# A sixth staging slot from a ring of x, and loads and small steps reordered, in an attention-plus-feed-forward kernel

## The chip, the cores and the metric

The kernel runs on one core of a Trainium2 chip. The metric is the device time of one execution in microseconds (us). Its engines are TensorE (PE, with weight loads shown as PEld), VectorE (DVE), ScalarE (ACT), GpSimd (POOL) and SyncE (SP), which only issues DMAs. Each works through its own instruction list in the order written; semaphores hold an instruction until what it needs is done.

## The reference

Eight batches, eight heads, 576 tokens, head size 64, all inputs float32. Attention without a score matrix gives x, and x goes through a feed-forward layer of 512 to 2048 to 512 with the activation h + sin(alpha h)^2 / alpha:

```
q_s = exp(q - max(q));   q_s /= sum over the 64 features
k_s = exp(k - max(k));   k_s /= sum over the 576 tokens
kv  = k_s^T @ v                      # 64 x 64 for each head
x   = (q_s @ kv), heads side by side # 4608 tokens x 512
h   = x @ w_in;  s = sin(alpha * h)
out = (h + s * s / (alpha + 1e-9)) @ w_out
```

## The kernel before

Each batch's 576 tokens are nine groups of 64 (the index j). The 4608 tokens of x are worked through as nine tiles of 512 tokens (t from 0 to 8). x stays on chip, transposed, in `xT`, which holds all 4608 tokens.

**A batch.** Its q, k and v are loaded in float32 into slots of the pool `stage`, five of them (`load`, `load_batch`). ACT takes exp of q and k (`exp_q`, `exp_k`, `exp_half`, L118). v is cast to bfloat16 into `vb` (`cast_v`, L137). `kv_mm` multiplies k and v on PE, `kv_norm` scales into `kbd` on DVE. `norm_q` sums q's features on DVE (L145, L150) and multiplies by the reciprocal into `qn` on POOL or DVE (L152). `qn` is transposed on PE (batches 0 and 1) or by DMA (`q_transpose_dma`, from batch 2). `attn_chunk` and `attn_out` multiply with `kbd`, and a cast on ACT or DVE puts x into `xT`.

**A tile.** `mm_h` makes one of 16 slices h of 512 tokens from four matmuls (L253); ACT takes the sine (L259); the square is taken by the engine that a letter in a string names (A for ACT, P for POOL, D for DVE); DVE's `combine` (L269) makes g; `mm_o` (L273) multiplies g with `wout`, and `evac_o` copies and stores. Banks of PSUM are handed out by letters too (`BANKS`). At most four s tiles exist at a time, so a sine waits for the combine four slices before it.

The order on every engine is the order in which the code is written (`tc.manual_schedule()`). All plain loads and stores are issued by SP, weights by POOL, which casts them on the way. A DMA issue on SP waits for the data that it needs and for an earlier DMA, eight issues before it.

**What is special at the start.** Tile 0 is batch 0's first eight groups and tile 1 is batch 1's. While tile 0's output is being multiplied (`o_quad`, four quarters of 16 matmuls, with `take(os, n)` issuing n of them), the code interleaves the attention of batch 1: exp of its two q halves, transposes after 46 output matmuls, `kv_mm` of both halves, `x_half`. The last quarter of `wout` is loaded in two pieces, slices 12 to 13 and 14 to 15; the latter is first needed by the 57th output matmul. The ninth groups of batches 0 and 1 are loaded alone into `q8` and normalized by `norm_q8`; in `o_stream(1)`, the output of tile 1, they are transposed and multiplied (L518 to L527) and become the first 128 tokens of tile 2. The rest of tile 2 is batch 2. Batch 3's v is loaded after batch 2's q transposes and cast by DVE ahead of tile 2's slices.

A dummy copy gates a DMA: a DVE or POOL copy that touches the target makes the load, which follows it on SP, wait; on POOL, a one-element copy `held` from a staged tile makes the weight loads behind it wait until that tile has landed.

Of the kernel before, what the change touches and what calls it, by code (L numbers as in the profile page):

```python
# [23 lines left out]
def kernel(  # L24
# [20 lines left out]
    J = 9  # L45
# [3 lines left out]
    nT = NT // MF  # L49
    BPT = MF // P  # L50
    NB = B * J

    ctx.enter_context(tc.manual_schedule())
    singles = ctx.enter_context(tc.tile_pool(name="singles", bufs=1))
    stage = ctx.enter_context(tc.tile_pool(name="stage", bufs=5))
    att1 = ctx.enter_context(tc.tile_pool(name="att1", bufs=1))
    att2 = ctx.enter_context(tc.tile_pool(name="att2", bufs=2))
    small = ctx.enter_context(tc.tile_pool(name="small", bufs=2))
# [5 lines left out]

    ident = singles.tile([128, 128], F32, name="ident")
    identb = singles.tile([128, 128], BF16, name="identb")
    xT = singles.tile([128, 4, NT], BF16, name="xT")
    q8 = singles.tile([128, 4, 2, D], F32, name="q8")
    win = singles.tile([128, 4, d_ff], BF16, name="win")
    wout = singles.tile([128, nN, dm], BF16, name="wout")  # L70
# [6 lines left out]
    def src_view(t, b):  # L77
        return t[b].rearrange("(i e) (p j) d -> (e p) i (j d)", e=2, j=J)
# [21 lines left out]
    def load_batch(b):  # L100
        load("q", q, b)
        load("k", k, b)
        load("v", v, b)
# [6 lines left out]
    def load_wout(n0, n1):  # L110
        nc.gpsimd.dma_start(out=wout[:, n0:n1, :], in_=wout_v[:, n0:n1, :])
# [27 lines left out]
    def norm_q(b, engs, j1=J):  # L139

        qe = A["qe", b][:, 0:j1].rearrange("p j (ii x d) -> p ii j x d", ii=2, x=2)
        A["qn", b] = qn = att1.tile([128, 2, J, 2 * D], BF16, name="qn")
        qs = small.tile([128, J, 4], F32, name="qs")
        if len(engs) == 1:
            nc.vector.tensor_reduce(qs, A["qe", b].rearrange("p j (i d) -> p j i d", i=4), axis=AXL.X, op=ALU.add)  # L145
            nc.vector.reciprocal(qs, qs)  # L146
        for ii in range(2):
            part = qs[:, 0:j1, 2 * ii:2 * ii + 2]
            if len(engs) == 2:
                nc.vector.tensor_reduce(part, qe[:, ii], axis=AXL.X, op=ALU.add)  # L150
                nc.vector.reciprocal(part, part)
            engs[ii % len(engs)].tensor_tensor(qn[:, ii, 0:j1].rearrange("p j (x d) -> p j x d", x=2), qe[:, ii],  # L152
                                               part.unsqueeze(3).to_broadcast([128, j1, 2, D]), op=ALU.mult)
# [62 lines left out]
    def attn_out(b, ii, half, pool, eng):  # L216
        qT, kt = A["qT", b], kbd[b % 2]
        j0, j1 = XO[half]
        n = (j1 - j0) * P
        xp = pool.tile([128, 2, 512], F32, name="xp", tag="a")  # L220
        for e in range(2):
            nc.tensor.matmul(xp[:, e, 0:n], kt[:, e, ii], qT[:, ii, j0:j1, e * 64:(e + 1) * 64],  # L222
                             start=True, stop=True)
        c0 = (J * b + j0) * P
        eng(xT[:, 2 * ii:2 * ii + 2, c0:c0 + n], xp[:, :, 0:n])  # L225

    def attn_chunk(b, c, j0, j1, xp):
# [18 lines left out]
    def mm_h(t, ni, k0=0, k1=4):  # L246

        if ni == 0 and k0 == 0:
            G[t] = gpool.tile([128, nN, MF], BF16, name="g")
        hp = HP[t, ni] if k0 else bank(BANKS.get(t, 4 * "aabb")[ni])  # L250
        HP[t, ni] = hp
        for ki in range(k0, k1):
            nc.tensor.matmul(hp, win[:, ki, ni * 128:(ni + 1) * 128],  # L253
                             xT[:, ki, t * MF:(t + 1) * MF], start=(ki == 0), stop=(ki == 3))
        return hp

    def sine(t, ni, hp, sq):
# [69 lines left out]
        vv = vb[0].rearrange("p j (i c) -> p i j c", i=4)  # L327
        eng(vv[:, 2 * ii:2 * ii + 2, j0:j1, 0:D], staged["v", 0][:, ii::2, j0:j1])

    GP_CP(singles.tile([128, 1], F32, name="held"), staged["k", 0][:, 0, 0, 0:1])  # L330
    load0(GP, "v", v, 1, 0, 5)
    load0(GP, "v", v, 1, 5, 9)
    for c0, c1 in ((0, 256), (256, 512), (512, 768), (768, 1024), (1024, 1536), (1536, 2048)):
# [42 lines left out]
    for c in range(2, 4):  # L376
        xp = bank("l")
        attn_chunk(0, c, 0, 8, xp)
        DVE_CP(xT[:, c, 0:MF], xp)
    for ki in range(2):  # L380
        for ni in range(2, 4):
            mm_h(0, ni, ki, ki + 1)
    for ni in range(4):
        mm_h(0, ni, 2, 3)

    def h_slot(t, ni, sq, lag):
        hp = mm_h(t, ni, 3 if t == 0 and ni < 4 else 2 if t == 1 and ni < 1 else 0)
        lag.append((t, ni, hp, sine(t, ni, hp, sq)))

    def flush(lag, keep):  # L390
        while len(lag) > keep:
            combine(*lag.pop(0))
# [17 lines left out]


    lag = []
    SQ = "PAPDPAPAPPDPAPAP"
    with ES:
        def load_q1():
            staged["q", 1] = st = stage.tile([128, 4, J, D], F32, name="st_q", tag="st")
            for ii in range(2):
                DVE_CP(st[:, ii, 0, 0:1], zero)
            for ii in range(2):
                nc.sync.dma_start(out=st[:, ii::2, 0:8].rearrange("p i j d -> p i (j d)"),  # L420
                                  in_=src_view(q, 1)[:, ii::2, 0:8 * D])

        def load_kv1():
            for n in "kv":
                staged[n, 1] = stage.tile([128, 4, J, D], F32, name=f"st_{n}", tag="st")
            DVE_CP(staged["k", 1][:, 0, 0, 0:1], zero)
            for ii in range(2):
                for n, t in (("k", k), ("v", v)):
                    nc.sync.dma_start(out=staged[n, 1][:, ii::2].rearrange("p i j d -> p i (j d)"),
                                      in_=src_view(t, 1)[:, ii::2])  # L430

        late = {6: load_q1, 8: lambda: load_wout(8, 12), 10: lambda: load_wout(12, 14), 13: load_kv1}
        for ni in range(nN):
            h_slot(0, ni, "DPPAPPAPPPAPPAPP"[ni], lag)
            flush(lag, 1)
            if ni in late:
                late[ni]()
        flush(lag, 0)

        accs = [bank(kind) for kind in "bbll"]  # L440
        os = o_quad(0, accs, [DVE_CP, ACT_CP, DVE_CP, DVE_CP])
        take(os, 46)
        for ii in range(2):
            exp_half("q", 1, ii, 8)
        norm_q(1, [GP, V], 8)
        load_wout(14, 16)
        for b in range(2):
            nc.sync.dma_start(out=q8[:, :, b], in_=src_view(q, b)[:, :, 8 * D:J * D])
        load_batch(2)

        def cast_v1(ii, eng):
            vv = vb[1].rearrange("p j (i c) -> p i j c", i=4)
            eng(vv[:, 2 * ii:2 * ii + 2, :, 0:D], staged["v", 1][:, ii::2])

        exp_half("k", 1, 0)
        cast_v1(0, ACT_CP)
        exp_half("k", 1, 1)
        q_tile(1)
        for ii in range(2):
            tp = ps_h[0].tile([128, 8, 128], BF16, name="tp", tag="a")  # L460
            q_transpose_ii(1, ii, 0, 8, tp)
            DVE_CP(A["qT", 1][:, ii, 0:8], tp)
        take(os, 4)

        def x_half(ii):
            xp = [bank("a") for _ in range(2)]
            for e in range(2):
                attn_chunk(1, 2 * ii + e, 0, 8, xp[e])
            for e in range(2):
                (ACT_CP, DVE_CP)[e](xT[:, 2 * ii + e, MF:2 * MF], xp[e])  # L470

        kv_mm(1, 0, ps_k, split=True)
        kv_norm(1, 0, 1)
        cast_v1(1, DVE_CP)
        take(os, 4)
        x_half(0)
        exp_to(A["qe", 1][:, J - 2:J], q8)
        take(os, 2)
        kv_mm(1, 1, ps_k, split=True)
        kv_norm(1, 1, 2)  # L480
        take(os, 4)
        x_half(1)
        nc.scalar.activation(zero, zero, AX.Sin)
        take(os)
        for ki in range(2):
            mm_h(1, 0, ki, ki + 1)
        norm_q8()
        load("q", q, 3)
        load("k", k, 3)

        for ni in range(nN):
            h_slot(1, ni, SQ[ni], lag)
            flush(lag, 1)
        cast_v(2, [GP_CP, GP_CP])
        flush(lag, 0)

# [14 lines left out]
    exp_q(2)  # L511
    exp_k(2)
    os = o_stream(1)
    take(os, 10)
    tp = ps_a.tile([128, 2, 2, 128], BF16, name="tp", tag="a")
    for b in range(2):
        for ii in range(2):
            nc.tensor.transpose(tp[:, ii, b], A["qe", 1][:, J - 2 + b, ii * 128:(ii + 1) * 128], identb)  # L518
    DVE_CP(A["qT", 1][:, :, J - 2:J], tp)
    take(os, 7)  # L520
    xp = ps_a.tile([128, 4, 2, P], F32, name="xp", tag="a")
    for c in range(4):
        ii, e = divmod(c, 2)
        for b in range(2):
            nc.tensor.matmul(xp[:, c, b], kbd[b][:, e, ii], A["qT", 1][:, ii, J - 2 + b, e * 64:(e + 1) * 64],
                             start=True, stop=True)
    DVE_CP(xT[:, :, 16 * P:18 * P], xp.rearrange("p c b n -> p c (b n)"))  # L527
    norm_q(2, [GP, V])
    exp_q(3)
    exp_k(3)  # L530
    q_transpose_dma(2, halves=True)
    load("v", v, 3)
    nc.scalar.activation(zero, zero, AX.Sin)
    take(os, 15)
    kv_mm(2, 0, ps_a)
# [14 lines left out]
    DVE_CP(xT[:, :, c0 + 6 * P:c0 + 9 * P].rearrange("p (h c) n -> p h c n", h=2),  # L550
           xp.rearrange("p h (c n) -> p h c n", c=2))
    take(os)
    cast_v(3, [DVE_CP, DVE_CP])
    q_transpose_dma(3)
    load_batch(4)

# [78 lines left out]
```

## Time and profile before

| what | value |
|---|---|
| median of 3 runs | 284.83 us (284.79 to 285.01) |
| the profiled execution | 285.96 us |
| its span, first to last instruction | 284.2 us |
| busy PE, DVE, ACT, POOL | 271.7, 193.0, 225.1, 82.3 us |
| granted PE clock | 1.00 throughout |
| HBM read, written | 36.71 MB, 9.44 MB |

The span is 1.76 us shorter than the profiled execution's own time, and that execution was 1.13 us above the median. In the profile's rows, "out<-in" are the program's tile names, "xN" counts the instructions, and a bracket at the end gives the idle time of the engine just before a row and what ended it. A matmul's shown end is modelled, and neighbouring matmuls overlap. SPq and POOL rows of DMA_DIRECT2D are issues, not transfers.

### The profile page before, as it was taken

How to read it: one execution, taken by the hardware profiler on the slowest of the kernel's cores; microseconds unless marked ns; L12 is line 12 of the kernel's file. 1: busy time of each engine (PE TensorE's matmuls, PEld its weight loads, DVE VectorE, ACT ScalarE, POOL GpSimd, SP SyncE). 2: the span in 40 equal slices, each digit the busy share in tenths (PEclk: the TensorE clock that was granted, in tenths of full speed). 3: DMA queues.
4: the chain of work that ended last, by engine and by line, in shares of the span. 5: the costliest groups of instructions: out<-in, count | busy, mean ns of one | idle time of the engine just before them, and what ended most of it. 6: DMA issues, size and time to landing. Idle time of an engine off the chain costs nothing.

```text
span 284.2 us, 4841 instructions
## 1 busy us (share of the span) xinstructions
PE 271.7 (96%) x1857; PEld 128.0 (45%) x1857; DVE 193.0 (68%) x287; ACT 225.1 (79%) x319; POOL 82.3 (29%) x78
## 2 busy tenths in 40 slices
PE   2899898999999999999999999999999999999995
PEld 1444354445444444444444444444444444444443
DVE  3957868989999768756785677667774555555412
ACT  4978847999479999899989998999877777777500
POOL 2979620674386650025002500341000000000000
PEclk9999999999999999999999999999999999999999
DMA  7999999951999119911991099118011111111143
GB/s 253 302 194 235 295 354 406 307 229 41 242 259 397 47 36 311 348 38 26 278 386 35 9 251 408 36 37 153 9 37 37 37 39 37 37 37 40 43 106 74
DMA packets 39127, 45.80 MB, mean 161 GB/s; under 512 B 17072, under 2 KB 22464, under 8 KB 39104
## 3 DMA queue, kind: packets, MB, share of 16 engines
q1 hardware_dynamic: 33360, 40.57, 45.9%
q0 software_dynamic: 5552, 4.79, 10.2%
q8 instruction: 14, 0.23, 0.3%
q10 hardware_dynamic: 192, 0.14, 0.2%
q14 instruction: 9, 0.07, 0.1%
HBM read 36.71 MB, written 9.44 MB: 162 GB/s over the span
## 4 chain that ended last, share of the span: by engine, by line
PE 71%; DMA 8%; ACT 7%; DVE 7%; issue 3%; POOL 3%; SPq 0%; POOLq 0%; ACTq 0%
PE hp L253 32%; PE op L273 32%; ACT s L259 4%; DMA wout<-in_moe_w_out_dram 3%; DVE g L269 2%; DMA st_v<-in_v_dram 2%; DMA win<-in_moe_w_in_dram 2%; DMA st_k<-in_k_dram 2%; PE xp L222 1%; DVE qs L150 1%; PE op L605 1%; PE lp L253 1%; POOL s L263 1%; DVE vb L137 1%; PE kvp L173 1%
## 5 line engine op out<-in xcount | busy, mean ns | idle before, releaser
L269 DVE SCALAR_TENSOR_TENSOR g<-s,inva_sb,hp 128x512 bf16<-128x512 f32 x128 | 94.3, 745 | 57.3 <-ACT s L261 53.1
L253 PE MATMUL hp<-xT,win 128*128 128x512 bf16 x512 | 128.3, 379 | 0.8 <-DMA win<-in_moe_w_in_dram 0.7
L273 PE MATMUL op<-wout,g 128*128 128x512 bf16 x496 | 124.4, 379 | 0.0
L259 ACT ACTIVATE s<-hp,alpha_sb 128x512 f32<-128x512 f32 x128 | 86.4, 683 | 24.0 <-PE hp L253 22.4
L253 PEld LDWEIGHTS <-win 128*128 128x128 bf16 x576 | 56.1, 98 | 68.3 <-issue 1.3
L273 PEld LDWEIGHTS <-g 128*128 128x128 bf16 x560 | 54.1, 98 | 62.7 <-issue 2.3
L261 ACT ACTIVATE s<-s 128x512 f32<-128x512 f32 x111 | 69.9, 630 | 3.5
L263 POOL TENSOR_TENSOR s<-s 128x512 f32<-128x512 f32 x30 | 32.4, 1095 | 22.3 <-ACT s L259 22.0
L152 POOL TENSOR_TENSOR qn<-qe,qs 128x1152 bf16<-128x1152 bf16 (+1 forms) x12 | 25.1, 2112 | 38.3 <-DVE qs L146 30.2
L285 DVE COPY o<-op 128x512 f32<-128x512 f32 (+2 forms) x33 | 22.1, 669 | 9.7 <-PE op L273 7.4
L137 POOL CAST vb<-st_v 128x1152 bf16<-128x1152 f32 x10 | 11.3, 1164 | 44.3 <-DMA st_v<-in_v_dram 44.3
L118 ACT ACTIVATE ke<-st_k 128x1152 bf16<-128x1152 f32 x16 | 17.9, 1151 | 3.8 <-DMA st_k<-in_k_dram 3.8
L118 ACT ACTIVATE qe<-st_q 128x1152 bf16<-128x1152 f32 (+1 forms) x16 | 17.5, 1129 | 2.5 <-DMA st_q<-in_q_dram 2.3
L145 DVE TENSOR_REDUCE qs<-qe 128x36 f32<-128x2304 bf16 x5 | 12.8, 2554 | 7.9 <-ACT qe L118 7.9
L225 DVE CAST xT<-xp 128x512 bf16<-128x512 f32 (+1 forms) x18 | 13.5, 750 | 0.0
L118 ACT ACT_TABLE_LOAD x7 | 9.0, 1283 | 1.3 <-PEq L619 1.2
L273 PE MATMUL lp<-wout,g 128*128 128x512 bf16 x32 | 8.9, 379 | 0.9 <-DVE g L269 0.9
L273 PE MATMUL hp<-wout,g 128*128 128x512 bf16 x32 | 8.9, 379 | 0.7 <-DMA wout<-in_moe_w_out_dram 0.7
L150 DVE TENSOR_REDUCE qs<-qe 128x16 f32<-128x1024 bf16 (+1 forms) x6 | 7.5, 1244 | 1.8 <-ACT qe L118 1.6
L222 PE MATMUL xp<-qT,kbd 128*128 128x256 bf16 (+1 forms) x40 | 8.2, 286 | 0.5 <-DVE xT L225 0.5
L173 PEld LDWEIGHTS <-ke 64*64 64x64 bf16 x576 | 5.8, 106 | 4.6 <-issue 1.6
L186 DVE TENSOR_TENSOR kbd<-kvp,kvr 64x256 bf16<-64x256 f32 (+1 forms) x20 | 7.4, 369 | 0.5
(83 smaller groups left out, 138.1 us busy)
## 6 DMA issues: line engine op xcount, KB each, us to landing
out_dram<-o SPq DMA_DIRECT2D x70, 128.0 KB, 2.4
st_q<-in_q_dram SPq DMA_DIRECT2D x6, 1152.0 KB, 6.4
st_k<-in_k_dram SPq DMA_DIRECT2D x6, 1152.0 KB, 9.0
st_v<-in_v_dram SPq DMA_DIRECT2D x6, 1152.0 KB, 11.3
st_k<-in_k_dram SPq DMA_DIRECT2D x4, 576.0 KB, 6.4
st_q<-in_q_dram SPq DMA_DIRECT2D x4, 512.0 KB, 6.0
st_v<-in_v_dram SPq DMA_DIRECT2D x3, 576.0 KB, 7.0
wout<-in_moe_w_out_dram POOLq DMA_DIRECT2D x3, 512.0 KB, 10.3
```

Source lines behind the costliest of these rows:

```text
L118: nc.scalar.activation(dst[:, :, ii * 128:(ii + 1) * 128].rearrange("p j (x d) -> p x j d", x=2), src[:, ii::2], AX.Exp)
L137: engs[ii](vv[:, 2 * ii:2 * ii + 2, :, 0:D], staged["v", b][:, ii::2])
L145: nc.vector.tensor_reduce(qs, A["qe", b].rearrange("p j (i d) -> p j i d", i=4), axis=AXL.X, op=ALU.add)
L152: engs[ii % len(engs)].tensor_tensor(qn[:, ii, 0:j1].rearrange("p j (x d) -> p j x d", x=2), qe[:, ii], part.unsqueeze(3).to_broadcast([12 ...
L225: eng(xT[:, 2 * ii:2 * ii + 2, c0:c0 + n], xp[:, :, 0:n])
L253: nc.tensor.matmul(hp, win[:, ki, ni * 128:(ni + 1) * 128], xT[:, ki, t * MF:(t + 1) * MF], start=(ki == 0), stop=(ki == 3))
L259: nc.scalar.activation(s, hp, AX.Sin, scale=alpha_sb[:, ni:ni + 1])
L261: nc.scalar.activation(s, s, AX.Square)
L263: nc.gpsimd.tensor_tensor(s, s, s, op=ALU.mult)
L269: nc.vector.scalar_tensor_tensor(G[t][:, ni], in0=s, scalar=inva_sb[:, ni:ni + 1], in1=hp, op0=ALU.mult, op1=ALU.add)
L273: nc.tensor.matmul(acc, G[t][:, ni, j * 128:(j + 1) * 128], wout[:, ni, :], start=(ni == 0), stop=(ni == nN - 1))
L285: eng(o[:, cols], acc)
```

## The change

- `xT` holds 2560 tokens, five tiles, and is written and read at the column modulo 2560. `stage` gets a sixth slot.
- Batch 3's v is loaded behind its k, ahead of tile 1's slices, and cast by POOL between its products for batches 2 and 3; before, DVE cast it ahead of tile 2.
- Batch 1: q's second half is issued after tile 0's slice 13, with k and v behind it (before, both halves after slice 6). k is no longer gated, since its slot is fresh. The last wout piece waits on POOL until the first half of k has landed.
- `q8` and batch 2's loads are issued after batch 1's q transposes, `q8` behind two DVE copies that touch it; exp of `q8` is moved behind the second `kv_norm`.
- The ninth groups' transposes, products and copies move from tile 1's output into tile 1's slices 11 and 14 (`late_q8`).
- Tile 0: ACT casts the fourth chunk of x, DVE the third; the third-quarter matmuls of slices 0 to 3 are issued with the fourth quarter instead of ahead of it. The squares of slices 9 and 15 go from POOL to ACT and DVE; in tile 1 that of slice 3 from DVE to POOL.

No matmul, activation or transfer is added or left out; four one-element gating copies became six.

```diff
+    NX = 5 * MF
-    stage = ctx.enter_context(tc.tile_pool(name="stage", bufs=5))
+    stage = ctx.enter_context(tc.tile_pool(name="stage", bufs=6))
-    xT = singles.tile([128, 4, NT], BF16, name="xT")
+    xT = singles.tile([128, 4, NX], BF16, name="xT")
...
-        c0 = (J * b + j0) * P
+        c0 = (J * b + j0) * P % NX
...
-                             xT[:, ki, t * MF:(t + 1) * MF], start=(ki == 0), stop=(ki == 3))
+                             xT[:, ki, t * MF % NX:t * MF % NX + MF], start=(ki == 0), stop=(ki == 3))
...
-        DVE_CP(xT[:, c, 0:MF], xp)
+        (DVE_CP, ACT_CP)[c - 2](xT[:, c, 0:MF], xp)
...
-    for ni in range(4):
-        mm_h(0, ni, 2, 3)
...
-        hp = mm_h(t, ni, 3 if t == 0 and ni < 4 else 2 if t == 1 and ni < 1 else 0)
+        hp = mm_h(t, ni, 2 if ni < (4, 1, 0)[min(t, 2)] else 0)
...
-    SQ = "PAPDPAPAPPDPAPAP"
+    SQ = "PAPPPAPAPPDPAPAP"
...
-        def load_q1():
-            staged["q", 1] = st = stage.tile([128, 4, J, D], F32, name="st_q", tag="st")
-            for ii in range(2):
-                DVE_CP(st[:, ii, 0, 0:1], zero)
-            for ii in range(2):
-                nc.sync.dma_start(out=st[:, ii::2, 0:8].rearrange("p i j d -> p i (j d)"),
-                                  in_=src_view(q, 1)[:, ii::2, 0:8 * D])
+        def load_q1(ii):
+            if ii == 0:
+                staged["q", 1] = stage.tile([128, 4, J, D], F32, name="st_q", tag="st")
+            st = staged["q", 1]
+            DVE_CP(st[:, ii, 0, 0:1], zero)
+            nc.sync.dma_start(out=st[:, ii::2, 0:8].rearrange("p i j d -> p i (j d)"),
+                              in_=src_view(q, 1)[:, ii::2, 0:8 * D])
...
-            DVE_CP(staged["k", 1][:, 0, 0, 0:1], zero)
...
-        late = {6: load_q1, 8: lambda: load_wout(8, 12), 10: lambda: load_wout(12, 14), 13: load_kv1}
+        late = {6: lambda: load_q1(0), 8: lambda: load_wout(8, 12), 10: lambda: load_wout(12, 14), 13: lambda: (load_q1(1), load_kv1())}
...
-            h_slot(0, ni, "DPPAPPAPPPAPPAPP"[ni], lag)
+            h_slot(0, ni, "DPPAPPAPPAAPPAPD"[ni], lag)
...
+        GP_CP(held, staged["k", 1][:, 0, 0, 0:1])
         load_wout(14, 16)
-        for b in range(2):
-            nc.sync.dma_start(out=q8[:, :, b], in_=src_view(q, b)[:, :, 8 * D:J * D])
-        load_batch(2)
...
             DVE_CP(A["qT", 1][:, ii, 0:8], tp)
+        for b in range(2):
+            DVE_CP(q8[:, 0, b, 0:1], zero)
+        for b in range(2):
+            nc.sync.dma_start(out=q8[:, :, b], in_=src_view(q, b)[:, :, 8 * D:J * D])
+        load_batch(2)
...
-        exp_to(A["qe", 1][:, J - 2:J], q8)
         take(os, 2)
         kv_mm(1, 1, ps_k, split=True)
         kv_norm(1, 1, 2)
+        exp_to(A["qe", 1][:, J - 2:J], q8)
...
         load("k", k, 3)
+        load("v", v, 3)
+
+        def late_q8(ni):
+            if ni == 11:
+                tp = ps_k.tile([128, 2, 2, 128], BF16, name="tp", tag="a")
+                for b in range(2):
+                    for ii in range(2):
+                        nc.tensor.transpose(tp[:, ii, b], A["qe", 1][:, J - 2 + b, ii * 128:(ii + 1) * 128], identb)
+                DVE_CP(A["qT", 1][:, :, J - 2:J], tp)
+            elif ni == 14:
+                xp = ps_k.tile([128, 4, 2, P], F32, name="xp", tag="a")
+                for c in range(4):
+                    ii, e = divmod(c, 2)
+                    for b in range(2):
+                        nc.tensor.matmul(xp[:, c, b], kbd[b][:, e, ii],
+                                         A["qT", 1][:, ii, J - 2 + b, e * 64:(e + 1) * 64], start=True, stop=True)
+                DVE_CP(xT[:, :, 16 * P:18 * P], xp.rearrange("p c b n -> p c (b n)"))
 
         for ni in range(nN):
             h_slot(1, ni, SQ[ni], lag)
             flush(lag, 1)
+            late_q8(ni)
...
-    take(os, 10)
-    tp = ps_a.tile([128, 2, 2, 128], BF16, name="tp", tag="a")
...
+    take(os, 17)
     norm_q(2, [GP, V])
     exp_q(3)
     exp_k(3)
+    cast_v(3, [GP_CP, GP_CP])
     q_transpose_dma(2, halves=True)
-    load("v", v, 3)
...
-    cast_v(3, [DVE_CP, DVE_CP])
     q_transpose_dma(3)
```

More of the change, by code (lines that the diff above doesn't have):

```diff
@@ L328, in cast_v0 @@
         eng(vv[:, 2 * ii:2 * ii + 2, j0:j1, 0:D], staged["v", 0][:, ii::2, j0:j1])
-    GP_CP(singles.tile([128, 1], F32, name="held"), staged["k", 0][:, 0, 0, 0:1])
+    held = singles.tile([128, 1], F32, name="held")
+    GP_CP(held, staged["k", 0][:, 0, 0, 0:1])
     load0(GP, "v", v, 1, 0, 5)
@@ L513 @@
     os = o_stream(1)
-    take(os, 10)
-    tp = ps_a.tile([128, 2, 2, 128], BF16, name="tp", tag="a")
[L516 to L527, printed above, removed]
+    take(os, 17)
     norm_q(2, [GP, V])
```

## Prediction

> **What bounds the kernel now.** I read the page first, then the stretch table, TensorE's waits, the timeline around each wait, and issue-to-landing times in the tile views.
>
> ```profile
> span 284.2 us, 4841 instructions
> PE 271.7 (96%) x1857; PEld 128.0 (45%) x1857; DVE 193.0 (68%) x287; ACT 225.1 (79%) x319; POOL 82.3 (29%) x78
> DMA  7999999951999119911991099118011111111143
> ```
>
> PE is the bound, and the DMA engines are full for the first fifth of the span. No matmul is removed, so only PE's gaps can pay.
>
> ```profile
> 28.00:31.00 3.00, 2.15 (x10) 0.87 (x9) 2.39 (x6) 2.65 (x5) 2.87 (x4) 1.00 1.12 323
> 31.00:46.00 15.00, 14.24 (x145) 6.99 (x145) 11.61 (x20) 8.30 (x10) 3.96 (x4) 1.00 1.11 344
> 46.00:61.00 15.00, 15.00 (x71) 6.81 (x70) 14.16 (x21) 14.23 (x24) 8.58 (x8) 1.00 0.97 355
> 105.00:134.00 29.00, 29.00 (x208) 13.74 (x206) 20.48 (x29) 27.18 (x40) 6.54 (x5) 1.00 0.56 180
> ```
>
> Columns: window and its length, busy PE, PEld, DVE, ACT, POOL, granted clock, DMA share, GB/s. From 105 us on PE has no gap and the clock is full, so the ring's later tiles can only lose. The gaps:
>
> ```profile
> 31.03 1.89 PE L273 MATMUL lp<-wout,g 128*128 128x512 bf16 x8 [0.88 <-DVE g L269]
> 44.66 1.02 PE L273 MATMUL hp<-wout,g 128*128 128x512 bf16 x4 [0.73 <-DMA wout<-in_moe_w_out_dram]
> 89.09 0.43 PE L222 MATMUL xp<-qT,kbd 128*128 128x320 bf16 x2 [0.49 <-DVE xT L225]
> 103.56 1.02 PE L253 MATMUL hp<-xT,win 128*128 128x512 bf16 x4 [0.17 <-DVE g L269]
> ...
> 28.15 4.20 POOL L263 TENSOR_TENSOR s<-s 128x512 f32<-128x512 f32 x4
> 28.30 0.69 ACT L259 ACTIVATE s<-lp,alpha_sb 128x512 f32<-128x512 f32 x1 [1.06 <-DVE g L269]
> ...
> 23.95 0.88 SPq L420 DMA_DIRECT2D st_q<-in_q_dram  x2
> 36.74 0.76 POOL L111 DMA_DIRECT2D wout<-in_moe_w_out_dram  x1
> 78.96 3.05 DVE L137 CAST vb<-st_v 128x1152 bf16<-128x1152 f32 x2 [0.41 <-DMA st_v<-in_v_dram]
> ```
>
> Four matmuls of 512 columns take 0.86 on the chain, 0.216 each, while one alone lasts 0.379 (group mean); a gap therefore costs its idle plus 0.16: 1.04, 0.89, 0.65 and 0.33. A fifth, about 0.30, is before the second chunk of batch 2's x at 74.20. That is 3.2 us in all, the most the change can bring.
>
> **The start of tile 0, 1.04.** The two x casts of chunks 2 and 3 ran one after the other on DVE (15.07, 1.29); now ACT takes the second, and the four third-quarter matmuls no longer run ahead of the first finished h. That h ends 3 x 0.216 = 0.65 earlier and ACT's first sine moves from 17.30 to 16.65, if the cast is done by 16.24 (ACT free at 15.45, cast 0.60). POOL loses squares 9 and 15 (1.04 each): its two wout issues (0.81 and 0.76) follow square 8 at 25.0 and end at 26.6. ACT is 0.65 earlier but has square 9 (0.63), so sine 11 still ends at 26.5; squares 11 and 12 run from 26.6 to 28.7, where before square 12 ended at 28.15 + 2 x 1.04 = 30.2. DVE's 0.75 combine then frees the l bank at 29.5. PE has 8 matmuls ahead of it from 28.26, until 29.99. The gap goes: -1.04. DVE pays 0.69 for square 15 at 30.4, hidden, since PE needs that result at 40.
>
> **q1's second half.** It moves from an issue at 24.36 to behind combine 12, about 29.7, past the two wout issues on POOL and directly ahead of k1 and v1 on SP. Before, the halves landed 6.5 and 8.9 us after issue, k1's first half 6.1 after 31.07, at 37.1. The engines move some 410 KB/us and were full, so the same bytes stand ahead of k1: k1 lands again near 37.1, and q1's half 1.4 us (576 KB) before it, 35.7, if in order of issue; if it shares with the cast-loads it takes twice its 1.28 us from 31.7, 34.3 (31.7 is 2 after the issue; a quiet transfer lands after 2.4). I take 35.0, since both ends are equally near. From there: exp 1.08, sum 1.20, reciprocal 0.25, product 1.23 (that at 7.11, alone on the port), handovers 0.25: 39.0. PE would reach those transposes at 28.26 + 46 x 0.216 + 0.45 for the first eight = 38.65: +0.35. Behind the wait on PE stand all of output quads and kv matmuls; SP has k1 and v1 behind the gate.
>
> The Trainium skill, "DMA: Bandwidth & Descriptors", section "Queues, rings and completion order", says each engine round-robins between queues per packet; alone that would give 34.3 and no stall, -0.35 on my sum. The trace is mixed: the earlier half needed 6.5 us with cast loads beside it.
>
> **wout's last quarter, 0.89.** POOL's new held copy (0.19) waits for k1's first half, 37.1, and then issues it: 37.3 against 36.74; behind it is only tile 1's first square, at 49. Before, it landed 7.9 us later with q8 and batch 2 queued beside it; now these are issued after the transposes of q1, by about 40.5, so it shares with v1's tail alone. Without them I allow 5 to 6 us (the quiet alpha load took 2.4, k1 6.1): 42.3 to 43.3, needed near 43.1 (43.77 before, less 0.7). Gap gone: -0.89; the late end would cost 0.2, and I charge 0.1.
>
> **q8 later.** Its gate stands behind the two qT copies on DVE (0.65 each), 40.3; SP issues at 40.5 and 41.0, with the batch 2 loads and tile 0's outputs behind. It took 10.2 before in the full queue; quiet transfers 2.4. I take 44.0 (3 after its issue, nearest the quiet row, since v1 is almost in). Then ACT: exp 0.72, o copy 0.59, xT cast 0.59, with handover 46.0. From those transposes (39.68) to tile 1's first matmul on that cast (47.24) PE took 7.56, 6.67 without the wout gap, so it wants the cast at 39.0 + 6.67 = 45.7: +0.3, or 0 to 1.3 from landings of 43.7 to 45. Exp of q8 itself is only moved. Sum up to tile 1: -1.04 +0.35 -0.89 +0.1 +0.3 = -1.2, bounds -1.9 to +2.0 (the last in the rivals).
>
> **The ninth groups in tile 1.** Four transposes and eight 64-column matmuls are moved, not added (0.39 and 0.40 busy, some 0.5 of PE). The matmuls at slot 14 need DVE's copy (0.42) queued behind combine 10, which ended at 59.85: ready at 60.3, PE there at about 60.0. That is +0.3, bounds 0 to 0.5. DVE also has the 0.68 xT copy, less 0.69 for square 3 (now POOL's, 1.04, in its 0.8 idle gaps). The last g is ready near 64.4, needed at 64.7: no charge, but without that cover 0.3.
>
> **v of batch 3.** Its load goes from 72.66, on SP behind the q transposes, to behind k3 near 54.5. Batch 2's loads end some 2 us later than before, so q3, k3 and v3 land near 61, 64 and 67; exp of q3 and k3 begin at 67.52 and 69.63, so nothing is late unless the delay passes 5 us. The casts leave DVE (3.05) for POOL (2 x 1.16) between qn of batches 2 and 3: POOL idles 6.0 there, cover enough. DVE's queue at 79 to 89 is shorter by 3.05, so the xT copy that ended the gap at 89.09 comes on time: -0.65. ACT lost 1.32 waiting on g at 82.76; it can run ahead, but ACT is 11.82 of 12 busy at 93 to 105, so of the 0.33 I count 0.2. The chain to the 74.20 gap loses its 0.68 xT copy: -0.2 of 0.30.
>
> One row speaks against POOL's casts: DVE's casts took 1.54 and 1.60 beside POOL, 0.77 alone at 42.45, and the q product 1.97 beside POOL's. The Trainium skill, "SBUF — State Buffer", section "SBUF: two separate sides", calls the pair's shared port an exclusive lock; by it both casts ahead of batch 2's product would cost 2.3 on the transposes. The cast at 78.96 ended at 80.50, 0.62 after POOL's running product (79.88) and ahead of POOL's next squares, so DVE was served first: I add 0 and keep 2.3 as the far bound (285.2).
>
> **Ring and slots.** A write into xT follows the last read of those columns by over four tiles; the sixth slot removes waits. Both 0; if that wait bit, PE from 105 on would show gaps.
>
> **Sum.** -1.2 +0.3 -0.65 -0.2 -0.2 = -1.95, say -1.9. The profiled execution took 285.96 (span 284.2 and 1.76 around it), 1.13 above the median; it would become 284.06, and the median 284.83 becomes 282.9.
>
> **Rivals.** (a) All five gaps go and nothing comes back: -3.2, 281.6. For it: PE's order is otherwise unchanged; against: three new waits with margins under 0.5. (b) The early gains are given back: q1's half lands at 36.6 or q8 at 45.2, leaving +0.3 -0.65 -0.2 -0.2 = -0.75: 284.1. For it: full DMA until 61. (c) Slower: q1's half keeps its old 8.9 from an issue at 29.7 and lands at 38.6. The transposes come at 42.6 and tile 1's cast matmul at 42.6 + 6.67 = 49.3, 2.0 late; less 0.75 later: +1.3, 286.1. It decides from a landing of 37.3 on (37.9 for 0.2%). Against: k1, issued after it, landed at 37.1 with the same bytes ahead. (d) The early v load collides with outputs and frees nothing: -1.2+0.3, 283.9, inside (b).
>
> **Chances.** Forecast 0.52, (a) 0.13, (b) with (d) 0.20, (c) 0.15. A measurement of this kernel tells about 0.2% (0.57 us) from no change. Of (b) a quarter, and of (c) a fifth, fall within it: faster 0.80, same 0.08, slower 0.12. The range 281.6 to 285.0 leaves out (c) and little else.
>
> **What would show it.** Right: no gap at the first lp output matmul nor at the last wout quarter; DVE without vb casts near 79; no xp gap at 89. Wrong: PE waiting over 1 us at the q1 transposes for DVE, ACT waiting on q8 past 45.2, or gaps beyond 105.

## The result, and the profile after

The changed kernel took 284.57 us (median of 14 runs, 284.03 to 284.95) against 285.49 for the kernel before, run beside it (14 runs, 284.79 to 286.86). The ratio is 0.9953, with a 95% interval of 0.9938 to 0.9968: 1.34 us less at the 284.83 of the first table, so 283.5 where 282.9 was forecast, inside the range. The ratio is not the quotient of the two medians: these lie 0.92 apart, which would make it 283.9. In a later set of runs (E13) the ratio was 0.9966 (0.9948 to 0.9984). Executions that were disturbed are left out of all ratios; the profile of one experiment fell into such an execution, so a second run of that kernel is shown for it.

The page and the stretch table of the changed kernel, the rows that answer to those shown of before:

```profile
span 282.8 us, 4815 instructions
PE 270.2 (96%) x1828; PEld 128.3 (45%) x1857; DVE 188.2 (67%) x285; ACT 226.0 (80%) x321; POOL 83.9 (30%) x80
DMA  7999999996589029811991099018011111111143
...
28.00:31.00 3.00, 3.00 (x15) 1.37 (x14) 2.75 (x7) 2.97 (x5) 1.35 (x2) 1.00 1.21 230
31.00:46.00 15.00, 13.98 (x142) 6.70 (x144) 10.74 (x22) 7.45 (x11) 2.86 (x3) 1.00 0.98 301
105.00:134.00 29.00, 28.74 (x185) 13.57 (x174) 20.54 (x30) 27.18 (x40) 6.48 (x4) 1.00 0.57 181
```

DVE is 4.8 us less busy: 3.05 of it are the two v casts that went to POOL, and most of the rest are the x cast that went to ACT (0.69) and a product for `q8` that took 0.69 instead of 1.52. The stretch from 28 to 31 has lost its gap. From 31 to 46 PE is busy for less, 13.98 where it had been 14.24. That alone shows no new wait, for this profile lacks 29 matmul records (1828 for 1857 weight loads), which lowers PE's busy time a little everywhere, from 105 us on too. PE's busy time can therefore not be compared with before; starts of named matmuls can. The timeline's rows at the old gaps and at the new waits:

```profile
29.73 1.89 PE L274 MATMUL lp<-wout,g 128*128 128x512 bf16 x8
43.48 1.04 PE L274 MATMUL hp<-wout,g 128*128 128x512 bf16 x4
87.59 0.43 PE L223 MATMUL xp<-qT,kbd 128*128 128x320 bf16 x2
102.18 1.02 PE L254 MATMUL hp<-xT,win 128*128 128x512 bf16 x4 [0.24 <-DVE g L270]
...
35.38 1.06 ACT L119 ACTIVATE qe<-st_q 128x1024 bf16<-128x1024 f32 x1 [3.86 <-DMA st_q<-in_q_dram]
38.01 1.22 DVE L153 TENSOR_TENSOR qn<-qe,qs 128x1024 bf16<-128x1024 bf16 x1
39.29 0.62 PE L203 MATMUL tp<-identb,qn 128*128 128x128 bf16 x8 [0.75 <-DVE qn L153]
44.20 0.72 ACT L119 ACTIVATE qe<-q 128x256 bf16<-128x256 f32 x2 [1.08 <-DMA q<-in_q_dram]
59.29 0.39 PE L506 MATMUL xp<-qT,kbd 128*128 128x64 bf16 x8 [0.18 <-DVE qT L500]
...
67.83 1.97 DVE L153 TENSOR_TENSOR qn<-qe,qs 128x1152 bf16<-128x1152 bf16 x1
68.53 3.39 POOL L138 CAST vb<-st_v 128x1152 bf16<-128x1152 f32 x2
```

The first three rows have lost the bracket that they had before; the fourth has kept its own. The second group is the chain of q1's second half: ACT waits for its landing, DVE's product ends at 39.23, and PE, which waited 0.75, starts the transposes at 39.29. Two waits are new: this one and the 0.18 at the ninth groups' products.

Counted by stage, from the first output matmul (28.26 before, 28.00 after, and 28.34 in a second profile of the changed kernel, so the start differs between executions) to the last matmul of the kernel:

| from, to | before | after | difference | forecast |
|---|---|---|---|---|
| first output matmul to second `kv_mm` of batch 1 | 15.18 | 15.07 | -0.11 | -1.04 +0.35 |
| to `kv_mm(2)` | 24.64 | 24.31 | -0.33 | -0.89 +0.1 +0.3 +0.3 |
| to `kv_mm(3)` | 14.20 | 13.92 | -0.28 | -0.2 |
| to `kv_mm(4)` | 23.75 | 23.34 | -0.41 | -0.65 -0.2 |
| to the last matmul | 174.37 | 174.38 | 0 | 0 |
| all | 252.14 | 251.02 | -1.12 | -1.93 |

A second profile of the changed kernel gave 251.06. This span of PE's work, "first output to last matmul", is used below for every run, since it leaves out the start. It is not free of it, though: where the output begins late, as in E2b below, the loads behind it have had more time.

### The profile page after: what moved, and what is told of

Same layout as the page of the kernel before. It is cut to its first block, busy times and chain, and to the rows that moved or that the text cites. A ratio compares the mean times of both kernels' runs of the same rounds, so it can differ in the third digit from the quotient of the medians.

```text
span 282.8 us, 4815 instructions
## 1 busy us (share of the span) xinstructions
PE 270.2 (96%) x1828; PEld 128.3 (45%) x1857; DVE 188.2 (67%) x285; ACT 226.0 (80%) x321; POOL 83.9 (30%) x80
## 3 DMA queue, kind: packets, MB, share of 16 engines
q0 software_dynamic: 5552, 4.79, 10.2%
## 4 chain that ended last, share of the span: by engine, by line
PE 79%; ACT 6%; DMA 5%; DVE 3%; POOL 2%; issue 2%; SPq 0%; ACTq 0%; POOLq 0%
PE op L274 37%; PE hp L254 34%; ACT s L260 3%; POOL s L264 2%; DMA st_v<-in_v_dram 2%; DMA st_q<-in_q_dram 2%; DVE g L270 2%; PE xp L223 2%; PE kvp L174 2%; PE op L611 1%; PE op L254 1%; DMA q<-in_q_dram 1%; ACT vb L329 1%; ACT qe L119 1%; SPq L299 0%
## 5 line engine op out<-in xcount | busy, mean ns | idle before, releaser
L274 PE MATMUL op<-wout,g 128*128 128x512 bf16 x478 | 121.6, 379 | 1.4 <-issue 0.6
L264 POOL TENSOR_TENSOR s<-s 128x512 f32<-128x512 f32 x29 | 30.6, 1067 | 20.2 <-ACT s L260 20.0
L138 POOL CAST vb<-st_v 128x1152 bf16<-128x1152 f32 x12 | 14.7, 1258 | 44.5 <-DMA st_v<-in_v_dram 44.5
```

The costliest lines, as they stand in the source:

```text
L138: engs[ii](vv[:, 2 * ii:2 * ii + 2, :, 0:D], staged["v", b][:, ii::2])
L264: nc.gpsimd.tensor_tensor(s, s, s, op=ALU.mult)
L274: nc.tensor.matmul(acc, G[t][:, ni, j * 128:(j + 1) * 128], wout[:, ni, :], start=(ni == 0), stop=(ni == nN - 1))
```

## The experiments

The theory: the gains are PE's removed gaps, and what is missing of the forecast is the new wait on q1's half and the kept gap at 102. The rivals: the loads' order gains nothing by itself and only the sixth slot pays; or the other way round. E1 to E4 ran on one chip, E5, E6, E9 and E10 on a second, E2b, E12, E13 and E14 on a third, each with the kernel before beside it. The changed kernel itself ran only for the result and as E13, so E3 to E10 are compared with it by the ratio and by PE's work in one profile each.

**E1: before, with the edits to tile 0 alone**

```diff
-        DVE_CP(xT[:, c, 0:MF], xp)
+        (DVE_CP, ACT_CP)[c - 2](xT[:, c, 0:MF], xp)
-    for ni in range(4):
-        mm_h(0, ni, 2, 3)
-        hp = mm_h(t, ni, 3 if t == 0 and ni < 4 else 2 if t == 1 and ni < 1 else 0)
+        hp = mm_h(t, ni, 2 if ni < (4, 1, 0)[min(t, 2)] else 0)
-            h_slot(0, ni, "DPPAPPAPPPAPPAPP"[ni], lag)
+            h_slot(0, ni, "DPPAPPAPPAAPPAPD"[ni], lag)
```

> The kernel before with the tile 0 edits alone: the fourth x chunk cast by ACT, the third-quarter matmuls issued with the fourth, squares of slices 9 and 15 off POOL. Gap accounting: the 1.04 us gap at the first lp output matmul goes, but the last wout piece still lands near 44 to 44.6, so PE waits there that much longer (idle 1.1 to 1.8 us instead of 0.73) and the time falls by 0 to 0.6 us (284.2 to 284.8 by the first median). Rival, each gap counts by itself: 1.04 us less, 283.8. Rival, only the early v load pays: the same gap returns at once in the next output quarter and the time does not move.

Measured: 285.51 against 285.46, ratio 0.9995 (0.998 to 1.0009); 251.99 from first output to last matmul. The gap at 31 was gone, and this took its place:

```profile
42.88 0.76 DVE L451 CAST vb<-st_v 128x1152 bf16<-128x1152 f32 x1 [1.62 <-DMA st_v<-in_v_dram]
43.79 0.48 PE L173 MATMUL kvp<-vb,ke 64*64 64x65 bf16 x36 [1.43 <-DVE vb L451]
```

The second half of batch 1's v landed at 42.86, and PE, 1 us earlier than before, waited 1.43 for it. Tile 0's edits alone show no gain: the loads are next. I had expected wout to be the late one; it was v.

**E2: before, with the ring, the sixth slot and batch 3's v early on POOL**

```diff
-    stage = ctx.enter_context(tc.tile_pool(name="stage", bufs=5))
+    stage = ctx.enter_context(tc.tile_pool(name="stage", bufs=6))
...
+        load("v", v, 3)
...
+    cast_v(3, [GP_CP, GP_CP])
-    load("v", v, 3)
-    cast_v(3, [DVE_CP, DVE_CP])
```

> The kernel before with the ring, the sixth slot, batch 3's v loaded behind its k and cast by POOL alone. Gap accounting: the gaps at 31.0 and 44.7 stay, the gap at 89.1 shrinks from 0.65 to about 0.15, the 74.2 gap (0.30) stays because the ninth groups' xT copy is still ahead of the q sums on DVE: -0.5 us, bounds -0.3 to -0.9. Rival, the early v load is what pays: the whole -1.4 us of the change is seen here. Rival, the ring costs: new waits on PE from 105 us on, time the same or up.

Measured: 284.75 against 285.46, ratio 0.9978 (0.9961 to 0.9995). For its profile the kernel ran once more (E2b), without repeats:

> The same kernel as in the second experiment, for its profile. Gap accounting: gaps at 31.0 (about 1.0 us) and at the last wout piece (about 0.9) as before, the one at 89 down to about 0.15, the one at 103 unchanged (0.3 to 0.4). Rival, the whole gain of the change: the early gaps are smaller too.

It took 285.85 in that one execution (span 284.1). The gap at 89 was gone: from `kv_mm(3)` to `kv_mm(4)` PE took 23.33, as in the changed kernel (23.34). The gap at 102 stayed, at 0.40. Its start differed:

```profile
22.54 1.67 PE L254 MATMUL hp<-xT,win 128*128 128x512 bf16 x7 [1.04 <-DMA win<-in_moe_w_in_dram]
44.50 0.48 PE L174 MATMUL kvp<-vb,ke 64*64 64x65 bf16 x36 [0.85 <-DVE vb L454]
```

PE waited 1.04 for w_in in tile 0, its first output matmul came at 29.44, and the gap at 31 did not arise at all; yet v's last half landed at 43.56, 1.9 later than in the profile of before (41.65), and cost 0.85. So the slot with the early v is worth some 0.2% by itself (0.63 us), and the start differs by more than that from one execution to the next (28.26 and 29.44).

This limits what can be said of the rivals. PE's work in E2b was 250.83, less than the changed kernel's 251.02, though its order at the start is that of before. The first two stages of the table together took 39.82 before, 39.38 and 39.44 in two profiles of the changed kernel, and 39.03 in E2b. E2's interval also overlaps both of the changed kernel's. So it is not shown, by the times or by these stages, that the new order at the start adds to what the slot with the early v gives; only the single waits that come and go in the profiles show its effect.

**E3: changed, with both halves of q1 after slice 6**

```diff
-        late = {6: lambda: load_q1(0), ..., 13: lambda: (load_q1(1), load_kv1())}
+        late = {6: lambda: (load_q1(0), load_q1(1)), ..., 13: load_kv1}
```

> The changed kernel with both halves of batch 1's q loaded after slice 6 again, k and v after slice 13 as before. Gap accounting: q's second half lands near 33, PE's wait of 0.92 us at the second set of q transposes goes, wout lands near 42.3 to 42.6 as it is needed, q8 is issued 0.9 us earlier too: 0.6 to 0.9 us less than the changed kernel, about 2.0 to 2.3 us less than before. Rival, the wait only moves to the k and v halves, which land no earlier: PE waits at kv matmuls or on wout, and the time stays that of the changed kernel within 0.3 us.

Measured: 285.06 against 285.46, ratio 0.9986 (0.997 to 1.0003); span of PE's work 251.86. The half landed at 32.71 and the wait at the transposes was gone. But the changed kernel has no gate on k: in the order on SP, the gate on q1's second half held k and v too. Without it they were issued 5 us earlier. k's halves landed at 35.55 and 39.61 (36.72 and 39.70 in the changed kernel), but v's last half landed later. The view of k's load line, then PE:

```profile
L428 SPq DMA_DIRECT2D st_k<-in_k_dram x2: 467/467/467, 24.2 to 25.3; - x2
DMA to landing us min/median/max: 11.3/12.8/14.4
...
43.60 0.48 PE L174 MATMUL kvp<-vb,ke 64*64 64x65 bf16 x36 [1.02 <-DVE vb L450]
```

v's last half landed at 42.67 (41.09 in the changed kernel, and 40.95 to 41.61 in the six profiles with its order of loads: its own two, E4, E5, E6 and E10). As an improvement this was a miss. It speaks for q1's lateness having bought the timely v, but from one profile of E3; E14 below has a v that is late by itself.

**E4: changed, with the ninth groups' products one slot later**

```diff
-            elif ni == 14:
+            elif ni == 15:
```

> The changed kernel with the ninth groups' eight products issued after slice 15 instead of slice 14. Gap accounting: PE's wait of 0.35 us for DVE's qT copy goes, since that copy ended 0.7 us before slice 15 is done: 0.2 to 0.35 us less than the changed kernel. Rival: DVE's xT copy now stands directly ahead of the last combine and PE waits for that g in tile 1's output: no gain, or 0.2 us more.

Measured: 284.02 against 285.46, ratio 0.9956 (0.9941 to 0.9972); PE's work 250.72, 0.32 less than the changed kernel (251.04, mean of its two profiles). PE no longer waited there, and nothing later was late: this wait was all of that step's price.

**E5: changed, without the held copy that delays wout's last piece**

```diff
-        GP_CP(held, staged["k", 1][:, 0, 0, 0:1])
```

> The changed kernel without POOL's held copy, so the last wout piece is issued behind POOL's product, near 35.3 instead of 37.0. Theory, the last half of v is what is late next and the wout piece shares the DMA engines with it: v's last half lands near 42 to 42.9 instead of 41.1, PE waits 0.5 to 1.2 us at the second kv matmuls, and the time rises by as much, to about 0.5 us under the kernel before. Rival, the order of these two does not matter since the bytes are the same: no wait there, time of the changed kernel within 0.2 us.

Measured: 284.89 against 285.4, ratio 0.9982 (0.9965 to 0.9999); PE's work 250.54. The piece was issued at 35.56 instead of 37.01 and landed at 42.27 instead of 42.30. Views of its load and of v's (the last half in each), E5 and then the changed kernel:

```profile
DMA to landing us min/median/max: 6.7/6.7/6.7
DMA to landing us min/median/max: 10.1/10.1/10.1
```

```profile
DMA to landing us min/median/max: 5.3/5.3/5.3
DMA to landing us min/median/max: 10.0/10.0/10.0
```

I had expected the piece to hold up v; it did not (v landed at 41.61). So in these two executions the gate moved the issue and hardly the landing. Whether it pays in time stays open: the profile shows no loss without it, and the interval of the ratio overlaps those of the changed kernel, taking in E13's 0.9966 but not the 0.9953 of the result.

**E6: changed, but DVE casts batch 3's v ahead of tile 2, as before**

```diff
-    cast_v(3, [GP_CP, GP_CP])
...
+    cast_v(3, [DVE_CP, DVE_CP])
```

> The changed kernel with batch 3's v still loaded early, but cast by DVE ahead of tile 2's slices as before. Theory, it is the two casts on DVE that hold up its queue: with v there at once they still run beside POOL (1.2 to 1.6 us each), and PE's gap before the second ninth-slice product near 87.6 is 0.5 to 0.7 us again instead of 0.14: 0.4 to 0.6 us slower than the changed kernel. Rival, the late landing of v (79.0 before) was the cause: no gap, time of the changed kernel.

Measured: 284.97 against 285.4, ratio 0.998 (0.9964 to 0.9996); PE's work 251.29. v was there long before, and the gap came back; from `kv_mm(3)` to `kv_mm(4)` PE took 23.66, 0.32 more than in the changed kernel, where 0.4 to 0.6 was expected:

```profile
77.11 3.53 DVE L138 CAST vb<-st_v 128x1152 bf16<-128x1152 f32 x2
87.71 0.43 PE L223 MATMUL xp<-qT,kbd 128*128 128x320 bf16 x2 [0.41 <-DVE xT L226]
```

With E2 this settles that gap: the cast in DVE's queue made it, not the late load. The early load only allows the cast to run on POOL at a time when POOL is free.

**E9: changed, q1's halves as in E3, and k gated after slice 13**

```diff
+            DVE_CP(staged["k", 1][:, 0, 0, 0:1], zero)
...
+        late = {6: lambda: (load_q1(0), load_q1(1)), ..., 13: load_kv1}
```

> The changed kernel with both halves of batch 1's q loaded after slice 6, and k gated by a DVE copy after slice 13, so k and v start where they did before. Theory: no wait at the q transposes (0.92 us before), v's last half lands near 41.5, its cast ends near 42.4 and PE, 0.9 us earlier, waits 0.2 to 0.4 us for it: 0.5 to 0.7 us less than the changed kernel. Rival, any order that lets q's half go early makes v's last half later by the same: PE waits 0.8 to 1.2 us at the second kv matmuls, no gain.

Measured: 284.36 against 285.4, ratio 0.996 (0.9945 to 0.9974); PE's work 250.70, 0.34 less than the changed kernel where 0.5 to 0.7 was expected. q1 cost nothing, v landed at 41.07, and the step that the change had hidden came out:

```profile
44.23 0.72 ACT L119 ACTIVATE qe<-q 128x256 bf16<-128x256 f32 x2 [1.86 <-DMA q<-in_q_dram]
45.96 0.59 PE L254 MATMUL kvp<-xT,win 128*128 128x512 bf16 x2 [0.34 <-ACT xT L473]
```

q8 landed at 44.12, as in the changed kernel (44.09), but PE was now there first; with the refill the wait costs 0.50.

**E10: changed, with E4's edit and a square of tile 2 moved from ACT to DVE**

```diff
-    SQ2 = "PAPPAPAPPAPAPPAP"
+    SQ2 = "PAPPAPAPPAPAPPDP"
```

> The changed kernel with the ninth groups' products behind slice 15, and tile 2's slice 14 squared by DVE instead of ACT. Theory: the xp wait (0.35 us) goes, and ACT, which was 0.6 us behind PE at the end of tile 2, starts the exps of batch 4 that much earlier, so PE's gap of 0.41 us near 102 goes: 0.6 to 0.75 us less than the changed kernel, some 2 us less than before. Rival, ACT's later exps wait for their loads or DVE for POOL: the 102 gap stays, 0.3 us less.

Measured: 285.18 against 285.4, ratio 0.998 (0.9962 to 0.9997); PE's work 251.72. The gap at 102 was gone, and a larger one stood ahead of it:

```profile
92.13 0.99 DVE L266 TENSOR_TENSOR s<-s 128x512 f32<-128x512 f32 x1 [1.65 <-ACT s L260]
95.22 0.59 PE L254 MATMUL hp<-xT,win 128*128 128x512 bf16 x2 [0.77 <-DVE xT L226]
```

The square waited 1.65 on DVE for ACT's sine, and behind it stood batch 3's last x cast, which PE wanted first. A miss.

**E12: the changes that the runs pointed to, together**

E9's edits, E4's slot, and the gate of `q8` behind the first of the two qT copies instead of the second:

```diff
             DVE_CP(A["qT", 1][:, ii, 0:8], tp)
-        for b in range(2):
-            DVE_CP(q8[:, 0, b, 0:1], zero)
+            for b in range(2) if ii == 0 else ():
+                DVE_CP(q8[:, 0, b, 0:1], zero)
```

> The changed kernel with q's second half loaded after slice 6 and k gated after slice 13, the ninth groups' products behind slice 15, and q8's gate behind the first of the two qT copies. Theory: the waits at the q transposes (0.9), at xp (0.35) and for q8 (0.5, seen where only the first was taken away) are all gone: 0.9 to 1.1 us less than the changed kernel, 2.2 to 2.5 us less than before. Rival, q8 issued earlier shares the DMA engines with the last wout piece and v: PE waits 0.3 to 0.6 us there, and half of that gain is lost.

**E14: E12, with two squares of tile 2 exchanged between ACT and POOL** (`SQ2 = "PAPPAPAPPAPAPAPP"`)

> The previous kernel, and in tile 2 the squares of slices 13 and 14 exchange engines: 13 on ACT, 14 on POOL. Theory: ACT no longer squares right before the last sine, batch 4's exps start some 0.6 us earlier and PE's gap of 0.41 us near 102 goes, without the DVE work that delayed batch 3's x: 0.3 to 0.4 us less than the previous kernel. Rival, POOL's squares of 14 and 15 follow each other and the casts of batch 4's v and its product behind them come 1 us later: no gain.

**E13: the changed kernel beside them**

> The changed kernel itself, beside the two above on one chip: 0.4 to 0.6% under the kernel before, with the waits of its first profile within 0.3 us (q transposes 0.9, xp 0.35, 102 us 0.41).

| run | median us | ratio to before (285.92) | PE's work |
|---|---|---|---|
| E12 | 284.18 | 0.994 (0.9915 to 0.9964) | 249.74 |
| E14 | 284.59 | 0.9957 (0.9935 to 0.9978) | 250.53 |
| E13 | 285.12 | 0.9966 (0.9948 to 0.9984) | 251.06 |

TensorE's waits over 0.2 in E12, from its waits view, and its stretch from 31 to 46:

```profile
PE hp L254 <- ACT xT L371: 0.3, 1, 0.3
PE hp L254 <- DVE g L270: 0.2, 1, 0.2
...
31.00:46.00 15.00, 14.74 (x146) 7.13 (x148) 11.84 (x23) 8.47 (x12) 2.86 (x3) 1.00 1.09 316
```

The first is in tile 0, ahead of the output; behind it only the gap at 101.78 is left. E12 has the lowest ratio and the shortest span of PE's work of all that ran. By the medians on the same chip it is 0.94 below the changed kernel, as forecast, but only 1.74 below the kernel before, where 2.2 to 2.5 was expected; the changed kernel beside it, E13, gained 0.34% instead of 0.4 to 0.6. The intervals of the two ratios overlap, and E12's output began late, at 28.89, so the size of that step is less sure than its mechanism, which E4 and E9 show one by one. In E14 the gap at 102 gave way to one at 91.98 (0.20, for an ACT cast of x), and from `kv_mm(3)` to `kv_mm(4)` PE took 23.35, as with the gap (23.34 in E12). The rest by which its span of PE's work is longer lies at the start: v's last half landed at 42.55 in that execution, and PE waited 0.4 for it and 0.30 for wout. Neither of the two other ways to share the squares out (E10, E14) gave a gain here: the wait only changed its place.

## Why the prediction was right, and where its terms were off

The direction and four of the five gaps went as forecast, and the mechanism, gaps of PE that go and smaller ones that come, is what the rows show. The sum was too large by 0.8 of 1.93. Of that, 0.44 lies in the first two stages of the table, where one profile of the kernel before was taken for its usual state (E2b shows how far another can lie from it), and 0.44 in the fourth, where the gap at 102 stayed; the third gained 0.08 more than forecast. By its steps:

- **The start of tile 0, -1.04: right in itself.** The gap went, and where q1's half is early too (E9, E12) the table's first stage took 14.14, 1.04 less than before. E1 shows that it pays only with the loads behind it, a condition that the sum held in q1's and wout's terms but not in v's: that v's last half could be late was nowhere in it. In the changed kernel it was not: it landed at 41.09, and DVE came to its cast at 42.08.
- **q1's second half, +0.35: mis-sized, 0.91.** The chain from landing to transposes was forecast at 4.0 and took 3.99 (35.30 to 39.29). The landing was 0.30 later than the 35.0 that I took, inside its bounds of 34.3 to 35.7, and PE was there at 38.38 instead of 38.65, because its first output matmul came at 28.00. So half of the 0.56 by which the charge was too small is the landing, and half is PE's earlier arrival. In the six profiles with this order of loads the charge was 0.48 (E5) to 0.96 (E10 and E13). Of the landing, the half way between two bounds was the weak point: a queue that shares evenly between the load and the cast-loads would have given 34.3 and no wait, the order of issue 35.7, and the landing was nearer to the latter. "DMA: Bandwidth & Descriptors" of the Trainium skill, section "Queues, rings and completion order", has each engine round-robin between queues; by that alone there was nothing to pay, and the 0.75 of idle time speaks against taking it for the landing of a transfer in a full queue.
- **wout's last quarter, -0.89 +0.1: the gap went, but it was worth 0.67.** The piece landed at 42.30, the early end of the forecast. The table's second stage takes 23.97 where neither this wait nor that of the ninth groups is present (E4, E12), and took 24.64 before. Counted between the starts of matmuls the wait was 0.81, and without it PE waits 0.12 at the next x matmuls (44.46) for DVE's `kbd`, which it had hidden. Why the piece came in time stays open. E5 shows that the held copy is not needed for it. That the loads taken out from beside it are the cause is argued and not tried alone, and E1 and E2b speak against it: these loads are still beside it there, and it landed 14.8 and 14.5 after the first output matmul, against 16.4 in the profile of before and 14.1 to 14.6 in the six with the changed order. In both of them PE waited for v instead, so which of the two is late differs between executions.
- **q8, +0.3: the step right, its charge hidden.** It landed at 44.09 (forecast 44.0) and ACT's cast ended at 45.88 (46.0), but PE wanted it only at 46.20 and not at 45.7: the transposes came at 39.29 instead of 39.0, because of q1's larger wait, and from there PE took 6.91 and not 6.67, because wout's gap was worth less than I had taken off. E9 took q1's wait away and the charge appeared, 0.50. The sum did have both waits in one line of time; the size of the earlier one decided whether the later one was paid, and that size was wrong.
- **The ninth groups, +0.3: right.** 0.35 by the changed kernel's rows (0.18 idle and the refill), 0.32 by E4. With wout's 0.67 this makes up the -0.33 of the table's second stage.
- **The gap at 74.20, -0.2: right,** -0.28 by the table's third stage. That stage took 13.91 to 14.00 in eight of the ten profiles with the ninth groups moved, and 14.12 and 14.09 in E1 and E2b, where they stay; in the other two, E3 and E10, PE waited for a transpose of q by DMA.
- **v of batch 3, -0.65: right, -0.53** from `kv_mm(3)` to the xp matmuls (6.81 to 6.28), where 0.14 of idle time stayed. E6 and E2 show the cast on DVE as its cause.
- **The gap at 103.56, -0.2: wrong, +0.12.** ACT's rows of before, then of the changed kernel, in the order of time:

```profile
82.76 0.69 ACT L259 ACTIVATE s<-op,alpha_sb 128x512 f32<-128x512 f32 x1 [1.32 <-DVE g L269]
93.76 0.67 ACT L259 ACTIVATE s<-hp,alpha_sb 128x512 f32<-128x512 f32 x1
```

```profile
80.69 0.69 ACT L260 ACTIVATE s<-op,alpha_sb 128x512 f32<-128x512 f32 x1 [0.22 <-DVE g L270]
83.11 0.69 ACT L260 ACTIVATE s<-hp,alpha_sb 128x512 f32<-128x512 f32 x1 [0.50 <-PE hp L254]
92.38 0.67 ACT L260 ACTIVATE s<-hp,alpha_sb 128x512 f32<-128x512 f32 x1
```

Counted from the start of `kv_mm(3)` (82.28 and 81.31), ACT's first of these sines moved from +0.48 to -0.62: a head start of 1.10, as argued. Then ACT ran into PE's h and waited 0.50, and its last sine ahead of the exps of batch 4 came at +11.48 before and +11.07 after: 0.41 left. But PE had gained 0.53 at the xp matmuls on the way. Against PE, ACT stood 0.12 later than before, and by this much the stretch from the xp matmuls to the gap grew (14.47 to 14.59). I had costed ACT's gain as though PE stayed where it was, and counted PE's own gain beside it.
- **POOL's casts, 0: right.** DVE's product took 1.97, as before, and POOL's two casts 3.39 instead of 2 x 1.16. The Trainium skill, "SBUF — State Buffer", section "SBUF: two separate sides", has the shared port as a lock for a whole instruction; the rows agree, and show that here POOL paid. The far bound of 2.3 was too far.
- **Ring and slots, 0: right.** The last stage of the table took 174.38, and 174.37 before.

Rival (b), the early gains given back, is half true: to `kv_mm(2)`, 0.44 is left of the 0.88 that the same terms add up to in the forecast, but through q1's wait and the smaller price of wout's gap, and not through a late q8; the 283.5 by the ratio lies midway between the forecast and its 284.1. (a) fell with q1 and 102. (c) would have needed a landing past 37.3. (d) fell with E2: the early v alone makes the kernel faster.

## What to carry to other kernels

A gap at a load in one profile is one draw: before pricing it, read a second profile, since in another execution another load may be the late one. Where a kernel's start is bound by loads, a gap taken away early shows the next late transfer, so forecast it as a list of landings against the moments at which they are wanted, with all waits in one line of time: a later wait inside an earlier one is free, and comes due when the earlier one is mended. Look what else stands behind a gate in the same queue before you move it; q1's gate also timed k and v. A head start given to a feeding engine closes a gap only as far as the bound engine does not gain as much itself, and handing one of its instructions to a neighbour closes it only if nothing urgent stands behind it there.

## What the runs showed of the hardware that was not expected

- The same issues land at different times from one execution to the next: in E9, E12 and E14, whose loads are issued in the same order up to there, v's last half landed 12.9, 13.0 and 14.0 after the first output matmul. At its first matmuls with w_in PE waited 0.67 for that load in the profile of before, and in both profiles of the changed kernel only 0.19, for a cast of x; 9 us later the run of E2's kernel waited 1.04 for w_in. Over all profiles v's last half landed between 40.95 (E6) and 43.56 (E2b), and the first output matmul came between 27.74 (E6) and 29.44 (E2b). A late start hides the early gaps, so gains there don't add up from one run to another.
- With k and v issued 5 us earlier beside the cast-loads, their last landing came 1.6 us later (E3) although k's first came 1.2 earlier, and with wout's piece issued 1.45 us earlier its landing stayed where it was (E5, 42.27 and 42.30). So here, in one execution each, an earlier issue into the full queue was not an earlier landing of what came last. Which of the transfers lost by it was not taken apart.
- A transfer that took 10.2 us in the full queue (q8's two loads) took 2.3 and 2.9 when it was issued after the rest had nearly come in: it was wanted no sooner, and left the full queue to others.
